# Experts 0 to 3 of a mixture of experts: one product of 448 columns where two products of 224 stood

## The chip, the cores and the metric

The kernel runs on one core of one Trainium2 chip. Its time is the device time in microseconds (us) of one execution; the figure quoted is the median of the runs, and a profiled execution of the same program gives the trace.

## What is computed

Three layers stand one behind the other: a bucketed attention, a mixture of 8 experts that gives each of 1,536 tokens to one expert, and a dense layer with an ELU. The change touches the second alone:

```python
def _moe_ref(x, w_gate, w_output_gate, w1, w2):
    logits = x @ w_gate
    e_idx = np.argmax(logits, axis=1)
    ...
    for e in range(E):
        mask = e_idx == e
        h = np.maximum(x[mask] @ w1[e], 0.0)
        ye = h @ w2[e]
        out[mask] = gate_w[mask, None] * eom[mask, e, None] * ye
    return out
```

There D = 512 and F = 1024, so w1[e] is 512 by 1024 and w2[e] is 1024 by 512. The gate factors are multiplied into the tokens before the experts.

## The kernel before

Every number that enters a matrix product is split in two, a high part rounded to the matmul's format (fp32r) and a low part that holds the rest. A product is then the sum of three: high weights by high tokens, high weights by low tokens, low weights by high tokens, all added up in one PSUM buffer.

The experts run one after the other (the loop at L1064), each on CAP = 224 columns of tokens. An expert's first layer, `moe_L1`, runs 8 times (f = 0 to 7), once for each block of 128 of its 1,024 hidden rows: 4 blocks of the inner dimension by three matmuls of 224 columns make one product of 12 matmuls. Its result lies in PSUM tile `hps` (3 buffers). ScalarE (ACT) writes its ReLU, rounded, to `hh` (L1040), and VectorE (DVE) writes the rest to `hl` (L1041). The second layer, `moe_L2`, runs 4 times (dc = 0 to 3), over 8 inner blocks each: 24 matmuls into PSUM tile `yps` (2 buffers), then ACT writes `x2h` (L1051) and DVE `x2l` (L1052). Its first product reads `hh` and `hl` of f = 7 in its last three matmuls.

The weights come in pieces of 128 by 1024 numbers, 8 to an expert. A piece is loaded into one of 6 buffers `wraw`, and `split_piece` makes its high part `wh` on ACT (L755) and its low part `wl` on DVE (L758). Program order alone sets where that stands: after every second `moe_L1` and after every `moe_L2` the piece 4 ahead is split. After dc = 1 and dc = 2 the next expert's tokens are transposed on TensorE (`xTp`, L1023) and split on ACT (L1025) and DVE (L1026). Each engine executes its own instructions in program order. From expert 4 on, DVE also has the narrowing of the last layer's weights (L693 to L697) among them; in experts 0 to 3 it does not. Expert 0's tokens are not made by `make_xT` but by `first_xT`, in two separate buffers.

Of the kernel before, what the change touches and what calls it, by code (L numbers as in the profile page):

```python
# [8 lines left out]
F32 = mybir.dt.float32  # L9
F32R = mybir.dt.float32r  # L10
BF16 = mybir.dt.bfloat16
I32 = mybir.dt.int32
AF = mybir.ActivationFunctionType
ALU = mybir.AluOpType
# [11 lines left out]
def kernel(  # L26
# [15 lines left out]
    nc = tc.nc  # L42
# [14 lines left out]
    CAP = 224  # L57
# [34 lines left out]
    FB1 = F // 128  # L92
    KD = DM // 128
# [675 lines left out]
    xT = {}  # L769
# [102 lines left out]
    for n in range(NQ + 3):  # L872
# [41 lines left out]
        if nx < NPAIR:  # L914
            if s % 3 and s < 9:
                late = prep(nx, s // 3 * 2 + s % 3 - 1)
            if s in v_at:
                i = v_at.index(s)
# [80 lines left out]
    x2h = x2_p.tile([128, KD, XW], F32R, name="x2h")  # L999
    x2l = x2_p.tile([128, KD, XW], F32R, name="x2l")  # L1000

    moe = ctx.enter_context(ExitStack())
    m1 = moe.enter_context(tc.tile_pool(name="m1", bufs=1, reuse_waits="tile"))
    ps_y = moe.enter_context(tc.tile_pool(name="ps_y", bufs=2, space=PSUM, reuse_waits="tile"))
    ps_x = moe.enter_context(tc.tile_pool(name="ps_x", bufs=2, space=PSUM, reuse_waits="tile"))
    ps_h = moe.enter_context(tc.tile_pool(name="ps_h", bufs=3, space=PSUM, reuse_waits="tile"))
# [6 lines left out]

    def make_xT(e, half):
        if half == 0:
            xT[e] = [m1.tile([128, KD, CAP], F32R, tag="xT" + x, name="xT" + x) for x in ("h", "l")]
        hi, lo = xT[e]
        t = xsl[e]
        ps = ps_x.tile([128, 2, 2, 128], F32, tag="x", name="xTp")
        for i in range(2):  # L1020
            dc = 2 * half + i
            for a in range(2):
                nc.tensor.transpose(ps[:, i, a, :], t[:, a, dc * 128:(dc + 1) * 128], ident)  # L1023
        pv = ps.rearrange("p i a q -> p i (a q)")[:, :, 0:CAP]
        nc.scalar.activation(hi[:, 2 * half:2 * half + 2], pv, AF.Copy)  # L1025
        nc.vector.tensor_tensor(lo[:, 2 * half:2 * half + 2], pv, hi[:, 2 * half:2 * half + 2], ALU.subtract)  # L1026

    hT = {}

    def moe_L1(e, f, pc):  # L1030
        if f == 0:
            hT[e] = [m1.tile([128, FB1, CAP], F32R, tag="h" + x, name="h" + x) for x in ("h", "l")]
        hi, lo = xT[e]
        wh, wl = (t.rearrange("p (c f) -> p c f", c=KD) for t in wsp[pc])
        fs = slice(f % 2 * 128, f % 2 * 128 + 128)
        ps = ps_h.tile([128, CAP], F32, tag="h", name="hps")
        for dc in range(KD):
            for i, (w, x) in enumerate(((wh, hi), (wh, lo), (wl, hi))):
                nc.tensor.matmul(ps, w[:, dc, fs], x[:, dc], start=(dc == 0 and i == 0), stop=(dc == KD - 1 and i == 2))  # L1039
        nc.scalar.activation(hT[e][0][:, f], ps, AF.Relu)  # L1040
        nc.vector.scalar_tensor_tensor(hT[e][1][:, f], ps, 0.0, hT[e][0][:, f], ALU.max, ALU.subtract)  # L1041

    def moe_L2(e, dc, pc, col):
        hi, lo = hT[e]
        wh, wl = (t.rearrange("p (c f) -> p c f", c=FB1) for t in wsp[pc])
        ps = ps_y.tile([128, CAP], F32, tag="y", name="yps")
        for f in range(FB1):
            for i, (w, x) in enumerate(((wh, hi), (wh, lo), (wl, hi))):
                nc.tensor.matmul(ps, w[:, f], x[:, f], start=(f == 0 and i == 0), stop=(f == FB1 - 1 and i == 2))  # L1049
        cols = bass.ds(col, CAP)  # L1050
        nc.scalar.activation(x2h[:, dc, cols], ps, AF.Copy)  # L1051
        nc.vector.tensor_tensor(x2l[:, dc, cols], ps, x2h[:, dc, cols], ALU.subtract)  # L1052

    more = "a count of some of the tokens"
    most = nc.values_load(
        tab[0:1, 2 * E:2 * E + 1], engines=[ENG.Pool], min_val=0, max_val=NT, skip_runtime_bounds_check_because=more
# [7 lines left out]
    for e in range(E):  # L1064
# [9 lines left out]
        for f in range(FB1):  # L1074
            pc = e * NP + f // 2
            moe_L1(e, f, pc)
            narrow_ops(1)
            if f == 1 and e + 1 < E:
                scale_xs(e + 1, (nc.gpsimd, nc.gpsimd))
            if f == 4 and e >= E - NG:  # L1080
                tids(e - E + NG)
            if f % 2:
                wsp.pop(pc)
                split_piece(pc + AHEAD)
                if e == E - 1 and f == 7:
                    split_w2(0)
                take_w2()
# [3 lines left out]
        for dc in range(KD):  # L1091
            pc = e * NP + 4 + dc
            moe_L2(e, dc, pc, off)
            narrow_ops(2)
            wsp.pop(pc)
            split_piece(pc + AHEAD)
            if e + 1 < E and dc in (1, 2):
                make_xT(e + 1, dc - 1)
            if e == E - 1 and dc == 2:
                split_w2(1)  # L1100
            take_w2()
            if dc == 2 and e + 2 < E:
                load_xs(e + 2)
# [16 lines left out]
    def ff_L1(hf, fb, j):  # L1120
        wh, wl = (t[:, 0].rearrange("p (c f) -> p c f", c=KD) for t in w2s[fb])
        c0 = hf * (NT // 2) + j * HC
        ps = ps_g.tile([128, HC], F32, tag="g", name="gps")
        for dc in range(KD):
            for i, (w, x) in enumerate(((wh, x2h), (wh, x2l), (wl, x2h))):
                nc.tensor.matmul(  # L1126
                    ps, w[:, dc], x[:, dc, c0:c0 + HC], start=(dc == 0 and i == 0), stop=(dc == KD - 1 and i == 2)
                )
        return ps
# [50 lines left out]
    for k in range(len(steps)):  # L1180
        for j in range(2):
            ps = ff_L1(*steps[k], j)
# [130 lines left out]
```

## Time and profile before

| what | value |
|---|---|
| time, median of 3 runs | 737.04 us (736.97 to 737.53) |
| the profiled execution | 736.89 us |
| its span, first to last instruction | 735.1 us |
| TensorE matmul (PE) busy | 714.1 us, 97% of the span |
| VectorE busy | 562.6 us, 77% |
| ScalarE busy | 400.3 us, 54% |
| granted TensorE clock, mean | 0.987 of full speed |

The page also cuts the span in 40 slices of 18.4 us, gives the chain of work that ended last, and lists the costliest groups of instructions. A matmul's duration of some 270 ns is the time from its start to its modelled end; matmuls overlap, so the time between two starts is what one costs. The same holds for ACT and DVE, where an instruction may start up to 0.1 us before the one ahead of it has ended.

### The profile page before, as it was taken

The numbers are of one execution on the slowest core, as the hardware profiler recorded it, in microseconds if no ns is written. First come the engines' busy times: TensorE is split into PE (matmuls) and PEld (weight loads), VectorE is DVE, ScalarE is ACT, GpSimd is POOL, SyncE is SP. The second block draws the span as 40 slices with busy tenths as digits, with TensorE's granted clock in tenths as the row PEclk, the third lists the DMA queues.
The fourth block names the chain that finished last, engine by engine and source line by source line (L and its number), as shares of the span: only waits on it lengthen the run. The fifth ranks groups of instructions, "written<-read, shape, count | busy, mean of one in ns | idle before, by whom it ended". The sixth has DMA issues, their size and how long they took to land.

```text
span 735.1 us, 13186 instructions
## 1 busy us (share of the span) xinstructions
PE 714.1 (97%) x4686; PEld 672.0 (91%) x4687; DVE 562.6 (77%) x1093; ACT 400.3 (54%) x807; POOL 206.9 (28%) x492
## 2 busy tenths in 40 slices
PE   7999999999999979999999999999999999999996
PEld 5899999999999969999999999889988999899995
DVE  5888988989889988666688987786778955964433
ACT  3887878888788855555556554333432223232221
POOL 7444444554446434202251345000000000000203
PEclk9899999999999989999999999999999999999998
DMA  8856768577682208976779997232122200000202
GB/s 189 190 112 151 186 155 207 130 171 183 159 216 90 88 0 261 290 229 181 222 236 248 219 280 201 82 104 69 58 77 68 86 1 1 1 0 1 86 1 89
DMA packets 108537, 97.76 MB, mean 133 GB/s; under 512 B 33416, under 2 KB 94472, under 8 KB 108464
## 3 DMA queue, kind: packets, MB, share of 16 engines
q1 hardware_dynamic: 106000, 90.44, 46.1%
q0 software_dynamic: 2304, 6.40, 2.3%
q8 instruction: 39, 0.64, 0.3%
q14 instruction: 34, 0.28, 0.1%
q10 hardware_dynamic: 160, 0.00, 0.0%
HBM read 64.15 MB, written 10.72 MB: 102 GB/s over the span
## 4 chain that ended last, share of the span: by engine, by line
PE 50%; issue 31%; DMA 9%; DVE 4%; ACT 3%; POOL 1%; SPq 1%; ACTq 0%; POOLq 0%; DVEq 0%
PE yps L1049 10%; PE hps L1039 10%; PE o L378 8%; PE t L362 7%; DMA out_dram<-part,tidt 6%; PE s L314 4%; PE s L315 4%; PE zps L229 2%; PE sp L454 2%; ACT p L342 1%; PE prep L203 1%; DMA tid_d<-tok,g_pi 1%; PE xTp L1023 1%; DMA qb<-qhi 1%; PE xacc L818 1%
## 5 line engine op out<-in xcount | busy, mean ns | idle before, releaser
L365 DVE TENSOR_TENSOR ptlo<-t,pthi 128x384 fp32r<-128x384 f32 x192 | 100.0, 548 | 25.9 <-ACT pthi L364 23.4
L342 ACT ACTIVATE p<-s,bi,sc 128x768 f32<-128x768 f32 x96 | 96.0, 1000 | 21.3 <-POOL bi L335 19.7
L364 ACT ACTIVATE pthi<-t 128x384 fp32r<-128x384 f32 x192 | 84.8, 497 | 25.8 <-PE t L362 24.8
L758 DVE TENSOR_TENSOR wl<-wraw,wh 128x1024 fp32r<-128x1024 f32 x63 | 77.0, 1224 | 21.2 <-ACT wh L755 16.1
L1138 ACT ACTIVATE gh<-ee 128x384 fp32r<-128x384 f32 x64 | 33.6, 525 | 108.4 <-DVE ee L1137 108.4
L333 DVE TENSOR_REDUCE nm<-s 128x1 f32<-128x768 f32 x96 | 91.0, 947 | 0.0
L1126 PE MATMUL gps<-x2h,vh 128*128 128x384 f32 x256 | 86.5, 338 | 0.0
L1126 PE MATMUL gps<-x2h,vl 128*128 128x384 f32 x256 | 86.2, 337 | 0.0
L1126 PE MATMUL gps<-x2l,vh 128*128 128x384 f32 x256 | 86.0, 336 | 0.0
L1174 POOL DMA_INDIRECT out_dram<-part,tidt x12 | 11.6, 965 | 258.6 <-DVE part L1170 256.8
L362 PE MATMUL t<-ident,p 128*128 128x128 f32 x576 | 80.9, 276 | 2.9 <-DVE ptlo L365 1.9
L314 PE MATMUL s<-ka,qa 128*128 128x384 f32 x192 | 74.5, 388 | 3.0 <-ACT p L342 2.2
L1156 PE MATMUL a<-vh,gl 128*128 128x512 f32 x192 | 75.4, 393 | 1.7 <-DVE gl L1139 1.5
L1156 PE MATMUL a<-vl,gh 128*128 128x512 f32 x192 | 75.5, 393 | 0.0
L1156 PE MATMUL a<-vh,gh 128*128 128x512 f32 x192 | 75.4, 393 | 0.0
L362 PEld LDWEIGHTS t<-ident,p 128*128 128x128 f32 x576 | 68.6, 142 | 6.8 <-DVE ptlo L365 2.3
L1049 PE MATMUL yps<-hh,wh 128*128 128x224 f32 x256 | 71.4, 279 | 0.0
L1135 ACT ACTIVATE ee<-gps 128x384 f32<-128x384 f32 x64 | 31.2, 487 | 72.6 <-PE gps L1126 72.4
L1049 PE MATMUL yps<-hl,wh 128*128 128x224 f32 x256 | 70.5, 275 | 0.0
L1049 PE MATMUL yps<-hh,wl 128*128 128x224 f32 x256 | 70.0, 273 | 0.0
L378 PE MATMUL o<-pthi,vst 128*128 128x384 f32 x192 | 68.1, 355 | 0.8 <-ACT osb L399 0.6
L315 PE MATMUL s<-kb,qb 102*128 102x384 f32 x192 | 66.0, 344 | 0.8 <-DMA qb<-qhi 0.8
(202 smaller groups left out, 1865.1 us busy)
## 6 DMA issues: line engine op xcount, KB each, us to landing
wraw<-in_moe_w_dram SPq DMA_DIRECT2D x64, 512.0 KB
w<-in_moe_w_in_dram SPq DMA_DIRECT2D x16, 512.0 KB
w<-in_moe_w_out_dram SPq DMA_DIRECT2D x16, 512.0 KB
ka<-khi SPq DMA_DIRECT2D x30, 192.0 KB
xs_d<-zt SPq DMA_DIRECT2D x8, 528.0 KB
xs<-xs_d SPq DMA_DIRECT2D x8, 528.0 KB
raw_q<-in_q_dram SPq DMA_DIRECT2D x16, 192.0 KB
raw_k<-in_k_dram SPq DMA_DIRECT2D x16, 192.0 KB
```

Source lines behind the costliest of these rows:

```text
L314: nc.tensor.matmul(ps[:, j, 0:HC], opnd[st, "qa"][:, cb], opnd[st, "ka"][:, sl], start=True, stop=False)
L315: nc.tensor.matmul(ps[:, j, 0:HC], opnd[st, "qb"][0:64 + MROWS, cb], opnd[st, "kb"][0:64 + MROWS, sl], start=False, stop=True,)
L333: nc.vector.tensor_reduce(nm, sps[n][:, :, 0:HC], AX.XY, ALU.max, negate=True)
L342: nc.scalar.activation(p.rearrange("p (a b) -> p a b", a=2), sps.pop(n)[:, :, 0:HC], AF.Exp, bias=bi, scale=sc, accum_out=sums[hd][:, c:c ...
L362: nc.tensor.transpose(ps[:, a, :], p[:, kt * 128:(kt + 1) * 128], ident)
L364: nc.scalar.activation(ho, ps, AF.Copy)
L365: nc.vector.tensor_tensor(lo[:, HALF * g:HALF * (g + 1), i * 128:(i + 1) * 128], ps, ho, ALU.subtract)
L378: nc.tensor.matmul(ops[m], vst[hd][:, kt, :], t[:, kt, :], start=(kt == 0 and x == 0), stop=(kt == NC - 1 and x == 1))
L758: fs = [lambda: eng.tensor_tensor(lo, r, hi, ALU.subtract)]
L1049: nc.tensor.matmul(ps, w[:, f], x[:, f], start=(f == 0 and i == 0), stop=(f == FB1 - 1 and i == 2))
L1126: nc.tensor.matmul(ps, w[:, dc], x[:, dc, c0:c0 + HC], start=(dc == 0 and i == 0), stop=(dc == KD - 1 and i == 2))
L1156: nc.tensor.matmul(ps, x[:, cs], w, start=(fb in first_fb and i == 0), stop=(fb in last_fb and i == 2))
```

## The change

In experts 0 to 3 the high and the low part of the tokens now lie in one tile, so that a high weight block can meet both in one matmul of 2 x 224 = 448 columns. The PSUM tile holds both halves, `ps[:, 0]` and `ps[:, 1]`; the low weight block goes into `ps[:, 0]` alone. Where three matmuls of 224 columns stood, there is one of 448 and one of 224. The two halves are then added: ACT copies `ps[:, 1]` to an SBUF tile `sum`, DVE adds `ps[:, 0]` to it, and only then follow the ReLU (or the copy) on ACT and the low part on DVE, both of them from `sum`. These last two (`rest`) are put on a list and issued at the next product, behind its copy and ahead of its add. After f = 7, and at the start of each second-layer product, the list is emptied at once.

Expert 0's first layer keeps the three matmuls, since its tokens lie in two buffers, and so do experts 4 to 7. The number of PSUM buffers is the same.

```diff
     def make_xT(e, half):
         if half == 0:
-            xT[e] = [m1.tile([128, KD, CAP], F32R, tag="xT" + x, name="xT" + x) for x in ("h", "l")]
+            t = m1.tile([128, 2, KD, CAP], F32R, tag="xT", name="xT")
+            xT[e], xB[e] = (t[:, 0], t[:, 1]), t
...
+    def settle(n):
+        while len(owed) > n:
+            owed.pop(0)()
+
+    def product(ps, w, x, n):
+        wh, wl = w
+        for k in range(n - 1):
+            nc.tensor.matmul(ps, wh(k), x[:, :, k], start=(k == 0), stop=False)
+            nc.tensor.matmul(ps[:, 0], wl(k), x[:, 0, k], start=False, stop=False)
+        nc.tensor.matmul(ps[:, 0], wl(n - 1), x[:, 0, n - 1], start=False, stop=False)
+        nc.tensor.matmul(ps, wh(n - 1), x[:, :, n - 1], start=False, stop=True)
+
+    def joined(ps):
+        t = m1.tile([128, CAP], F32, tag="sum", name="sum", bufs=4)
+        nc.scalar.activation(t, ps[:, 1], AF.Copy)
+        settle(0)
+        nc.vector.tensor_tensor(t, ps[:, 0], t, ALU.add)
+        return t
...
+        if e in JOIN and e in xB:
+            ps = ps_h.tile([128, 2, CAP], F32, tag="h", name="hps2")
+            product(ps, (lambda k: wh[:, k, fs], lambda k: wl[:, k, fs]), xB[e], KD)
+            t = joined(ps)
+
+            def rest():
+                nc.scalar.activation(h, t, AF.Relu)
+                nc.vector.scalar_tensor_tensor(l, t, 0.0, h, ALU.max, ALU.subtract)
+
+            owed.append(rest)
+            if f == FB1 - 1:
+                settle(0)
+            return
...
+        if e in JOIN:
+            ps = ps_y.tile([128, 2, CAP], F32, tag="y", name="yps2")
+            settle(0)
+            product(ps, (lambda k: wh[:, k], lambda k: wl[:, k]), hT[e], FB1)
+            t = joined(ps)
+
+            def rest():
+                nc.scalar.activation(x2h[:, dc, cols], t, AF.Copy)
+                nc.vector.tensor_tensor(x2l[:, dc, cols], t, x2h[:, dc, cols], ALU.subtract)
+
+            owed.append(rest)
+            return
...
+    JOIN = (0, 1, 2, 3)
```

On ACT, in the first layer of expert 3, four products (f = 4 to 7) and two pieces of weights stand so before the change (`x2` marks two in a row):

```order
L1040 ACTIVATE hh<-hps 128x224 x2
L755 ACTIVATE wh<-wraw 128x1024
L1040 ACTIVATE hh<-hps 128x224 x2
L755 ACTIVATE wh<-wraw 128x1024
L1051 ISA
```

and so after it (the numbers behind the names tell one product's tile from another's):

```order
L1047 ACTIVATE sum<-hps_5484 128x224
L1064 ACTIVATE h<-sum 128x224
L1047 ACTIVATE sum<-hps_5498 128x224
L1064 ACTIVATE h<-sum 128x224
L755 ACTIVATE wh<-wraw 128x1024
L1047 ACTIVATE sum<-hps_5518 128x224
L1064 ACTIVATE h<-sum 128x224
L1047 ACTIVATE sum<-hps_5532 128x224
L1064 ACTIVATE h<-sum 128x224 x2
L755 ACTIVATE wh<-wraw 128x1024
```

Two instructions stand where one stood, and the ReLU `h` behind a copy belongs to the product before; the last two ReLUs stand together. On DVE the same stretch, before:

```order
L1041 SCALAR_TENSOR_TENSOR hl<-hps,hh 128x224 x2
L758 TENSOR_TENSOR wl<-wraw,wh 128x1024
L1041 SCALAR_TENSOR_TENSOR hl<-hps,hh 128x224 x2
L758 TENSOR_TENSOR wl<-wraw,wh 128x1024
L1052 ISA
```

and its end after the change, f = 5 to 7:

```order
L1049 TENSOR_TENSOR sum<-hps_5226,sum 128x224
L758 TENSOR_TENSOR wl<-wraw,wh 128x1024
L1065 SCALAR_TENSOR_TENSOR h<-sum,h 128x224
L1049 TENSOR_TENSOR sum<-hps_5246,sum 128x224
L1065 SCALAR_TENSOR_TENSOR h<-sum,h 128x224
L1049 TENSOR_TENSOR sum<-hps_5260,sum 128x224
L1065 SCALAR_TENSOR_TENSOR h<-sum,h 128x224
L758 TENSOR_TENSOR wl<-wraw,wh 128x1024
```

Behind each `wl` the low part of the product before comes first, then the next product's add. (These are expert 2's rows; experts 1 to 3 read alike.)

## Rows read from the trace of the kernel before

**Rows 1.** Windows: length, then PE, PEld, DVE, ACT, POOL busy, clock, DMA share, GB/s

```profile
325.46:347.77 22.31, 22.31 (x203) 22.31 (x202) 15.21 (x23) 12.73 (x22) 4.57 (x2) 1.00 0.69 214
370.08:392.40 22.32, 22.32 (x202) 22.32 (x202) 19.96 (x36) 12.74 (x22) 9.65 (x8) 1.00 0.76 199
...
460.00:560.00 100.00, 98.70 (x497) 88.91 (x496) 75.98 (x147) 36.25 (x68) 0.00 (x0) 1.00 0.25 77
560.00:700.00 140.00, 139.57 (x704) 126.44 (x703) 92.82 (x178) 39.80 (x75) 6.36 (x12) 1.00 0.08 27
```

**Rows 2.** Chain of work that ended last, expert 2: start, length, what

```profile
325.46 10.72 PE hps L1039 x96
336.18 5.36 PE yps L1049 x48
341.55 0.44 PE xTp L1023 x4
341.98 2.68 PE yps L1049 x24
```

**Rows 3.** Waits from 303 to 437 us: total, times, longest

```profile
ACT x2h L1051 <- PE yps L1049: 32.8, 24, 1.4
ACT hh L1040 <- PE hps L1039: 23.6, 24, 1.0
```

**Rows 4.** Timeline of PE, experts' stage and last layer: start, length, what

```profile
325.30 0.28 PE L1039 MATMUL hps<-xTh,wh 128*128 128x224 f32 x1
...
522.15 0.33 PE L1126 MATMUL gps<-x2h,vh 128*128 128x384 f32 x1
...
524.24 0.39 PE L1156 MATMUL a<-vh,gh 128*128 128x512 f32 x1
...
526.31 0.33 PE L1126 MATMUL gps<-x2h,vh 128*128 128x384 f32 x1
```

**Rows 5.** Timeline of ACT, expert 1's end and expert 2's start

```profile
322.64 1.05 ACT L755 ACTIVATE wh<-wraw 128x1024 fp32r<-128x1024 f32 x1
323.59 0.54 ACT L1025 ACTIVATE xTh<-xTp 128x448 fp32r<-128x448 f32 x1
325.50 0.36 ACT L1051 ACTIVATE x2h<-yps 128x224 f32 x1 [1.37 <-PE yps L1049]
...
328.18 0.36 ACT L1040 ACTIVATE hh<-hps 128x224 fp32r<-128x224 f32 x1 [0.98 <-PE hps L1039]
328.43 1.05 ACT L755 ACTIVATE wh<-wraw 128x1024 fp32r<-128x1024 f32 x1
```

**Rows 6.** Timeline of DVE, first layers of experts 0 and 2

```profile
284.17 0.68 DVE L1041 SCALAR_TENSOR_TENSOR hl<-hps,hh 128x224 fp32r<-128x224 f32 x2
...
328.57 0.39 DVE L1041 SCALAR_TENSOR_TENSOR hl<-hps,hh 128x224 fp32r<-128x224 f32 x1 [0.21 <-ACT hh L1040]
329.51 1.23 DVE L758 TENSOR_TENSOR wl<-wraw,wh 128x1024 fp32r<-128x1024 f32 x1 [0.55 <-PE hps L1039]
330.66 0.38 DVE L1041 SCALAR_TENSOR_TENSOR hl<-hps,hh 128x224 fp32r<-128x224 f32 x1
```

**Rows 7.** Timeline of DVE and of ACT, last layer: ACT waits for DVE

```profile
601.67 0.56 DVE L1137 SCALAR_TENSOR_TENSOR ee<-gps,ee 128x384 f32<-128x384 f32 x1
...
602.26 0.52 ACT L1138 ACTIVATE gh<-ee 128x384 fp32r<-128x384 f32 x1 [1.02 <-DVE ee L1137]
```

**Rows 8.** Windows of 2 us ahead of the experts and in expert 0 (columns of rows 1)

```profile
270.00:272.00 2.00, 0.04 (x2) 0.00 (x0) 1.93 (x9) 0.29 (x2) 0.50 (x1) 1.00 0.00 0
272.00:274.00 2.00, 1.72 (x15) 1.72 (x15) 1.86 (x12) 1.62 (x4) 0.41 (x1) 0.65 0.00 0
274.00:276.00 2.00, 2.00 (x11) 2.00 (x11) 1.90 (x7) 1.69 (x3) 1.84 (x2) 0.50 0.03 8
...
284.00:286.00 2.00, 1.66 (x15) 1.47 (x14) 2.00 (x5) 0.62 (x2) 0.00 (x0) 1.00 0.99 305
```

More of the change, by code (lines that the diff above doesn't have):

```diff
@@ L1026, in make_xT @@
         nc.vector.tensor_tensor(lo[:, 2 * half:2 * half + 2], pv, hi[:, 2 * half:2 * half + 2], ALU.subtract)
+    xB = {}
     hT = {}
+    owed = []
+    def settle(n):
[14 more added lines that the diff above has]
+        return t
     def moe_L1(e, f, pc):
         if f == 0:
-            hT[e] = [m1.tile([128, FB1, CAP], F32R, tag="h" + x, name="h" + x) for x in ("h", "l")]
-        hi, lo = xT[e]
+            hT[e] = m1.tile([128, 2, FB1, CAP], F32R, tag="h", name="h")
         wh, wl = (t.rearrange("p (c f) -> p c f", c=KD) for t in wsp[pc])
         fs = slice(f % 2 * 128, f % 2 * 128 + 128)
+        h, l = hT[e][:, 0, f], hT[e][:, 1, f]
+        if e in JOIN and e in xB:
[9 more added lines that the diff above has]
+            return
+        hi, lo = xT[e]
         ps = ps_h.tile([128, CAP], F32, tag="h", name="hps")
@@ L1039, in moe_L1 @@
                 nc.tensor.matmul(ps, w[:, dc, fs], x[:, dc], start=(dc == 0 and i == 0), stop=(dc == KD - 1 and i == 2))
-        nc.scalar.activation(hT[e][0][:, f], ps, AF.Relu)
-        nc.vector.scalar_tensor_tensor(hT[e][1][:, f], ps, 0.0, hT[e][0][:, f], ALU.max, ALU.subtract)
+        nc.scalar.activation(h, ps, AF.Relu)
+        settle(0)
+        nc.vector.scalar_tensor_tensor(l, ps, 0.0, h, ALU.max, ALU.subtract)
     def moe_L2(e, dc, pc, col):
-        hi, lo = hT[e]
         wh, wl = (t.rearrange("p (c f) -> p c f", c=FB1) for t in wsp[pc])
+        cols = bass.ds(col, CAP)
+        if e in JOIN:
+            ps = ps_y.tile([128, 2, CAP], F32, tag="y", name="yps2")
+            settle(0)
+            product(ps, (lambda k: wh[:, k], lambda k: wl[:, k]), hT[e], FB1)
[5 more added lines that the diff above has]
+            return
         ps = ps_y.tile([128, CAP], F32, tag="y", name="yps")
         for f in range(FB1):
-            for i, (w, x) in enumerate(((wh, hi), (wh, lo), (wl, hi))):
-                nc.tensor.matmul(ps, w[:, f], x[:, f], start=(f == 0 and i == 0), stop=(f == FB1 - 1 and i == 2))
-        cols = bass.ds(col, CAP)
+            for i, (w, x) in enumerate(((wh, 0), (wh, 1), (wl, 0))):
+                nc.tensor.matmul(
+                    ps, w[:, f], hT[e][:, x, f], start=(f == 0 and i == 0), stop=(f == FB1 - 1 and i == 2)
+                )
         nc.scalar.activation(x2h[:, dc, cols], ps, AF.Copy)
+        settle(0)
         nc.vector.tensor_tensor(x2l[:, dc, cols], ps, x2h[:, dc, cols], ALU.subtract)
+    JOIN = (0, 1, 2, 3)
     more = "a count of some of the tokens"
```

## The prediction

> **What bounds the kernel now.** I read the windows first, cut at the experts' borders: what counts is whether TensorE ever stands still in the stretch that is changed. In expert 2 PE is busy for 22.31 of 22.31 us, in expert 4, which keeps its form, for 22.32 of 22.32, and in the last layer for 98.70 of 100 and 139.57 of 140 us [rows 1]. The chain of work that ended last says the same from the other side: an expert is 10.72 us of first layer, 4 x 2.68 us of second layer and 2 x 0.44 us of transposes, all of it PE, 22.31 us together [rows 2]. The waits show the others waiting for PE: of nine rows none has PE waiting, none has ACT or DVE waiting for a load, and the longest with them as waiters are ACT's for PE [rows 3]. So PE is the bound from expert 1 to the end; what the change adds to or takes from an expert reaches the end of the kernel one to one, whichever engine it comes from. ACT is busy for 12.73 us of an expert and DVE for 15.21 [rows 1].
>
> **What the product gains on PE.** A matmul of 224 columns now costs 10.72/96 = 0.1117 us [rows 2]. What 448 columns cost no row shows; it is read between two sizes that stand in the last layer: 12 of 384 columns from 522.15 to 524.24, 0.174 us each, and 9 of 512 from 524.24 to 526.31, 0.230 us each [rows 4]. The line through both gives 0.202 us at 448 and 0.104 at 224. The 224 columns cost more than the line, and transposes of 128 columns cost 0.44/4 = 0.11 us as well [rows 2], so below some 240 columns it is not the columns that set the pace but, I take it, the weight load that comes with each matmul. The change takes one load in three away. A pair then costs 0.202 + 0.112 = 0.314 us where three matmuls cost 0.335: 0.021 us less, 0.085 in a first-layer product (4 pairs, 1.255 us), 0.17 in a second-layer product (8 pairs, 2.51 us), 0.68 in a half expert. Bounds of a pair: 0.335 (nothing gained) and, with 448 columns at one a cycle of the granted 2.4 GHz (clock 1.00 in rows 1), 0.187 + 0.112 = 0.299.
>
> The Trainium skill ("TensorE: Matmul & The Clock Gate", sections "Back-to-back issue gap" and "LDWEIGHTS (loading the stationary operand)") gives N/2.4 + 2.5 ns for a matmul and 128/1.2 = 107 ns for a load, so 0.189 + 0.107 = 0.296 us for a pair, an estimate from that page. For the load the trace is close (0.11); for 384 and 512 columns, where the page has 0.163 and 0.216, the rows have 0.174 and 0.230. By the page's pair the sum below would be 1.8 us lower.
>
> **What it adds on ACT and DVE.** Each joined product gets a copy on ACT (as `x2h`, 0.36 us) and an add on DVE (as `hl`, 0.39) [rows 5, 6]. By totals that fits: 12.7 + 12 x 0.36 = 17.1 us on ACT and 15.2 + 12 x 0.39 = 19.9 on DVE, under the 20.9 us that PE would need. By order it does not. Products now go ACT, DVE, ACT, DVE instead of ACT, DVE, and the split of a weight piece stands in the same two queues. The prices: on ACT the next instruction starts 0.25 us after a small one (328.18 to 328.43) and a split `wh` takes 1.05 [rows 5]; on DVE the next starts 1.15 after a `wl` (329.51 to 330.66) and 0.68 - 0.39 = 0.29 after a small one [rows 6]; ACT to DVE takes 0.03 (328.54 to 328.57) [rows 5, 6] and DVE to ACT 0.03 (602.23 to 602.26) [rows 7].
>
> In the first layer, from one even ReLU to the next but one (f = 0, 2, 4, 6): ReLU of f, 0.25; `wh` behind it on ACT, 1.05; hand over, 0.03; `wl`, 1.15; low part of f+1, 0.29; add of f+2, 0.39; hand over, 0.03; then ReLU of f+2. That is 3.19 us for two products. PE would need 2.51, and needs 2.68 today. So the first layers of experts 1 to 3 are no longer bound by PE but by this ring; today it does not exist, since `hh` waits only for PE.
>
> **The sum for experts 1 to 3.** Time 0 is the first matmul of the first layer. ACT sees the end of the product before at 0.20 (325.30 to 325.50 [rows 4, 5]): copy at 0.20, `wh` 0.45 to 1.50, `wl` at 1.53, the low part owed at 2.68, add of f = 0 at 2.97 to 3.36, its ReLU at 3.39. Three rounds of 3.19 bring the ReLU of f = 6 to 12.96. Its low part follows at 13.35, the add of f = 7 at 13.64, its ReLU at 14.06, its low part at 14.45, done at 14.84. The last matmul of the first second-layer product needs it: 0.03 to hand over, 0.11 to load, 0.20 to stream, so the second product starts at 15.18. Today it is 10.72 + 2.68 = 13.40: **1.78 us later**. PE stands in the meantime, first for an `hps` buffer (three, freed by the adds: f = 5 and f = 7 wait, 0.3 and 0.7 us), then for `h` of f = 6 and 7 (0.8 us each). The other three second-layer products have time: 2.51 us on PE against 1.15 + 2 x 0.29 + 0.53 (`xTl`) on DVE. They gain 3 x 0.17 = 0.51. Net +1.27 us for each of three experts, **+3.81**.
>
> **Expert 0** joins only its second layer, whose hidden rows come from the old form; it gains 4 x 0.17 = **-0.68**. Later experts run as before: the last product's owed copy and subtraction fall into gaps that ACT and DVE have. Loads see an expert that is longer, not shorter, so nothing there comes late. The swapped order of a product's last two matmuls costs nothing. Sum: +3.13 us on the profiled 736.89, 740.0; the median lies 0.15 above that run, so **740.2**.
>
> The open prices: 104 pairs run free of the ring (3 x 24 and 32), so a pair's bounds move the sum by -1.6 and +2.2 us. Some 12 handovers lie on an expert's path; at 0 or 0.06 us instead of 0.03 they move it by 0.36 each way, 1.1 for three. Both together reach from 737.5 to 743.5.
>
> **The rivals.** (1) *PE keeps the bound.* If ACT and DVE let ring and splits overlap better than their rows show, seven half experts gain 0.68 each: 4.8 us, 732.2. For it speak the totals, 17.1 and 19.9 under 20.9 us; against it, that every step of the ring is a wait for data or a place in a queue. It decides once the ring takes less than 2.51 us, a fifth less than the rows add up to. 8%. (2) *448 columns run at the bare column rate*, a pair at 0.299: -1.6 on the forecast, 738.6, with cheaper handovers down to 737.5. Rows at 384 and 512 columns speak against it. 15%. The page's two rules above are this case, at 738.3. (3) *The change does not do what it says:* the second load was never the limit, or two token blocks in one matmul cost extra, and a pair stays at 0.335. Then +2.2, 742.4. 8%. (4) *The clock falls* where PE now waits. After 270 to 272 us, with 0.04 us of work, the clock was 0.65 and 0.50 in the next two windows, 1.2 GHz for some 3.4 us; in 284 to 286, with 1.66 us of work, it stayed at 2.4 GHz [rows 8]. The new gaps are below 1 us each, nearer to the second row. If it fell once in each of experts 1 to 3, half the speed for 3.4 us would cost 1.7 us each: 745.3. 7%.
>
> **How the numbers follow.** The forecast has 62%. The range, 737.3 to 743.6, takes in rivals 2 and 3 and leaves out 1 and 4, 15%. A measurement of this kernel can tell 0.2%, 1.5 us, from no change. Faster: rival 1 and a little of the low ends, 0.09. Same, up to 738.5: half of rival 2 and the forecast's low edge, 0.14. Slower: 0.77.
>
> **What would show it.** In experts 1 to 3 of the changed kernel: 23.6 us from one first layer to the next; ReLUs of even f 3.2 us apart; PE waiting for DVE, 2 to 3 us an expert, most of it in the first second-layer product; 448-column matmuls whose pair takes 0.314 us where nothing waits; expert 0's second layer 0.7 us shorter; experts 4 to 7 at 22.3; clock 1.00 throughout. An expert of 20.9 us with no PE wait would make it wrong.

## The result and the profile after

The changed kernel takes **741.66 us** (median; 740.71 to 742.4) beside 737.0 for the kernel before on the same chip (736.36 to 737.53): a ratio of **1.0063**, 95% interval 1.005 to 1.0076. That is 4.66 us slower. The forecast was 740.2 with a range of 737.3 to 743.6, so sign and range hold, and the size is short by a third.

Windows of the changed kernel, cut at the first matmul of each expert's first layer, experts 0 to 4 (columns as in [rows 1]):

```profile
280.76:303.28 22.52, 22.18 (x171) 21.37 (x170) 17.82 (x27) 14.89 (x26) 5.26 (x6) 1.00 0.98 288
303.28:327.18 23.90, 22.51 (x138) 20.05 (x137) 18.82 (x35) 16.21 (x34) 4.13 (x2) 1.00 0.71 215
327.18:351.30 24.12, 22.38 (x137) 20.04 (x136) 18.81 (x35) 16.15 (x34) 3.47 (x2) 1.00 0.64 196
351.30:375.43 24.13, 22.39 (x138) 20.06 (x136) 18.81 (x35) 16.15 (x34) 3.63 (x2) 1.00 0.65 197
375.43:397.73 22.30, 22.30 (x202) 22.30 (x200) 20.66 (x38) 12.99 (x23) 8.42 (x8) 1.00 0.79 203
```

Experts 1 to 3 take 23.90, 24.12 and 24.13 us, 72.15 together, where the kernel before takes 22.31 for each, 66.93 (expert 2 in [rows 2]; experts 1 and 3 read alike): **+5.2**. Expert 0 takes 22.52 where it took 23.1 (279.89 to 302.99 in PE's timeline of before): **-0.6**. All of that lies in its second layer, 11.01 us instead of 11.58; its first layer takes 11.5 in both traces, though up to 12.55 in the traces of kernels below that leave it as it is. Expert 4 keeps its three matmuls, and its time too, although in the changed kernel its tokens and hidden rows also lie in joined tiles, as those of experts 5 to 7 do; so the tiles by themselves cost nothing there. The two differences make +4.6, nearly the whole change of the median. (The profiled execution took 742.4, and its experts start 0.87 us later than in the trace of before, ahead of anything that was changed.) No engine is full in experts 1 to 3: PE is busy for 22.4 of 24.1 us, DVE for 18.8, ACT for 16.2. What bounds such a stretch is an order of waits, and the chain shows it.

Chain of work that ended last in the changed kernel, expert 2, one round of the first layer and the tail behind it (start, length, what; "issue" is time in which the engine waited for nothing that the profile shows):

```profile
337.27 0.03 ACT h L1064
337.30 0.27 issue
337.57 1.05 ACT wh L755
338.62 0.02 issue
338.64 1.23 DVE wl L758
339.87 0.30 DVE h L1065
340.17 0.31 DVE sum L1049
340.49 0.02 issue
340.51 0.40 ACT h L1064
...
341.66 0.40 ACT h L1064
342.06 0.02 issue
342.08 0.40 DVE h L1065
...
342.53 0.47 PE yps L1043
```

Where [rows 2] have nothing but PE, PE comes in here only at 342.53. The ring of the prediction stands there link by link: ReLU, `wh`, `wl`, low part, add, and the next even ReLU 3.24 us later. The even ReLUs of the whole first layer (ACT's timeline, same expert):

```profile
330.64 0.39 ACT L1064 ACTIVATE h<-sum 128x224 fp32r<-128x224 f32 x1 [0.31 <-DVE sum L1049]
...
333.87 0.39 ACT L1064 ACTIVATE h<-sum 128x224 fp32r<-128x224 f32 x1 [1.03 <-DVE sum L1049]
...
337.27 0.39 ACT L1064 ACTIVATE h<-sum 128x224 fp32r<-128x224 f32 x1 [1.29 <-DVE sum L1049]
...
340.51 0.39 ACT L1064 ACTIVATE h<-sum 128x224 fp32r<-128x224 f32 x1 [1.12 <-DVE sum L1049]
```

Rounds of 3.23, 3.40 and 3.24 us, each ended by a wait for DVE's add. In [rows 3] ACT waits for PE alone. The round of 3.40 has one longer split in it (DVE's timeline):

```profile
332.01 1.23 DVE L758 TENSOR_TENSOR wl<-wraw,wh 128x1024 fp32r<-128x1024 f32 x1 [0.26 <-ACT wh L755]
...
335.25 1.38 DVE L758 TENSOR_TENSOR wl<-wraw,wh 128x1024 fp32r<-128x1024 f32 x1 [0.27 <-ACT wh L755]
```

PE's timeline of the changed kernel shows what a pair costs and where PE stands (same expert):

```profile
330.97 0.36 PE L1040 MATMUL hps<-xT,wh 128*128 128x448 f32 x1
331.17 0.26 PE L1041 MATMUL hps<-xT,wl 128*128 128x224 f32 x1
331.27 0.38 PE L1040 MATMUL hps<-xT,wh 128*128 128x448 f32 x1
...
332.23 0.37 PE L1040 MATMUL hps<-xT,wh 128*128 128x448 f32 x1
...
333.99 0.45 PE L1040 MATMUL hps<-xT,wh 128*128 128x448 f32 x1 [0.33 <-DVE sum L1049]
...
337.39 0.45 PE L1040 MATMUL hps<-xT,wh 128*128 128x448 f32 x1 [0.64 <-DVE sum L1049]
...
341.38 0.47 PE L1040 MATMUL yps<-h,wh 128*128 128x448 f32 x1 [0.57 <-DVE h L1065]
```

From 330.97 to 332.23 four pairs run without a wait, 0.315 us each. Then PE waits for an `hps` buffer and at last for `h`.

### The profile page after: what moved, and what is told of

It is laid out like the page before. It is cut to its first block, busy times and chain, and to the rows that moved or that the text cites. A ratio compares the mean times of both kernels' runs of the same rounds, so it can differ in the third digit from the quotient of the medians.

```text
span 740.7 us, 12841 instructions
## 1 busy us (share of the span) xinstructions
PE 712.9 (96%) x4462; PEld 663.2 (90%) x4463; DVE 573.8 (77%) x1133; ACT 411.9 (56%) x847; POOL 207.1 (28%) x492
## 4 chain that ended last, share of the span: by engine, by line
PE 41%; issue 31%; DMA 10%; DVE 8%; ACT 6%; POOL 2%; SPq 2%; ACTq 0%; POOLq 0%; DVEq 0%
PE o L378 7%; DMA out_dram<-part,tidt 6%; PE t L362 6%; PE hps L1075 5%; PE yps L1098 4%; PE s L314 4%; PE s L315 3%; PE yps L1040 2%; DVE wl L758 2%; ACT wh L755 2%; PE zps L229 2%; ACT p L342 2%; PE sp L454 2%; PE yps L1041 1%; SPq L132 1%
## 5 line engine op out<-in xcount | busy, mean ns | idle before, releaser
L755 ACT ACTIVATE wh<-wraw 128x1024 fp32r<-128x1024 f32 x63 | 66.0, 1051 | 0.7 <-DMA wraw<-in_moe_w_dram 0.5
L378 PE MATMUL o<-ptlo,vst 128*128 128x384 f32 x192 | 64.9, 338 | 0.0
L778 POOL TENSOR_SCALAR xs<-xs 128x512 f32<-128x512 f32 x14 | 29.3, 2103 | 115.0 <-DMA xs<-xs_d 115.0
```

The source lines that it names most:

```text
L378: nc.tensor.matmul(ops[m], vst[hd][:, kt, :], t[:, kt, :], start=(kt == 0 and x == 0), stop=(kt == NC - 1 and x == 1))
L755: eng_hi.activation(hi, r, AF.Copy)
```

## The experiments

The theory is the ring: a joined product goes to ACT, DVE, ACT and DVE, and with the split of a weight piece in the same two queues it comes round too late for PE. The rivals: the joined matmuls themselves cost more (load, columns, PSUM); GpSimd or the total load of VectorE does it. The kernels were run in three groups, each beside runs of the kernel before, whose medians were 737.38, 737.75 and 736.95; each ratio is to those of its own group.

### Each half alone

The second layer alone:

```
-        if e in JOIN and e in xB:
+        if False:
```

> Only the second layers of experts 0 to 3 are joined; the first layers keep three matmuls of 224 columns and two evacuation steps. Ring theory (the loss sits in the first layers, where copy, ReLU and weight split on ScalarE and low part, add and weight split on VectorE wait for each other in turn): no ring, PE without a wait, four half experts gain 4 x 0.17 us each, 16 x 0.17 = 2.7 us less than before: 734.3 us. Load theory (VectorE and ScalarE simply have too much to do): 4 x 0.39 us more on VectorE, 16.8 us of some 21.6, also no loss. Rival that joining itself costs (the matmul over two token blocks, the adds): 737 or above.

Measured: 734.58 (734.42 to 734.62), ratio 0.9961, 0.9947 to 0.9974. The window of expert 1 (2 and 3 read alike):

```profile
302.46:324.18 21.72, 21.72 (x170) 21.13 (x169) 16.24 (x27) 13.86 (x26) 4.85 (x2) 1.00 0.82 247
```

As expected of it (734.3). PE has no idle time again, and an expert takes 0.59 us less than before: 32 pairs, 0.0185 us each. So the joined product does save time on PE, and the loss must come from the first layer. The first layer alone:

```
-        if e in JOIN:
+        if False:
```

> Only the first layers of experts 1 to 3 are joined; all second layers keep their three matmuls. Ring theory: the first layer and the first second-layer product take 15.4 to 15.7 us as in the changed kernel, where 13.4 stood before, and nothing is gained in the other second-layer products: 2.0 to 2.3 us more for each of three experts, 743.1 to 743.8 us, slower than the full change. Load theory: 8 x 0.39 us more on VectorE, 18.3 of 22.3 us, fits: about 735.

Measured: 742.59 (742.5 to 743.38), ratio 1.0074, 1.006 to 1.0088; experts 1 and 2 take 24.04 and 24.22 us (expert 3 24.20). The ring had put it at 743.1 or above, the load at 735: the ring theory holds, half a microsecond milder. The two halves do not add up. Joining the second layer saves 0.59 us an expert by itself, but behind a joined first layer only 0.14 and 0.10 us (23.90 and 24.12 against 24.04 and 24.22). ACT's timeline of this kernel shows the first ReLU of expert 2:

```profile
330.12 0.39 ACT L1064 ACTIVATE h<-sum 128x224 fp32r<-128x224 f32 x1
```

That is 3.10 us behind the first matmul (327.02); in the changed kernel it is 3.46 (327.18 to 330.64). There the last second-layer product owes DVE a low part, and `x2l` stands ahead of the add:

```profile
329.92 0.38 DVE L1091 TENSOR_TENSOR x2l<-sum,x2h 128x224 f32 x1
330.22 0.39 DVE L1049 TENSOR_TENSOR sum<-hps,sum 128x224 f32<-128x224 f32 x1
```

That puts 0.30 us ahead of the ring, and 0.06 more come from ACT's first copy, which starts 0.26 us after the first matmul (327.18 to 327.44) instead of 0.20 (327.02 to 327.22), behind a last matmul of 448 columns instead of 224. So 0.36 us of what PE gains in three second-layer products goes into the start of the next ring.

### Two products owed instead of one

If the ring binds, letting the ReLU and the low part of a product come one product later takes the add out of their line, with the same instructions:

```
-    def joined(ps):
+    def joined(ps, n=0):
...
-        settle(0)
+        settle(n)
...
-            t = joined(ps)
+            t = joined(ps, 1)
```

(The last line is the first layer's call.)

> The full change, with one number altered: in the first layer the ReLU and the low part of a product are issued two products later instead of one (until f = 7, where all are issued). The same instructions on every engine, in another order. Ring theory: the ReLU of f waits for an add that was done a whole product earlier, so the ring spans three products instead of two and its 3.2 us fit in 3 x 1.25; PE is the bound again but for the end at f = 7, an expert takes 21.3 to 21.4 us: 3.5 us less than before, 733.5 us. Load theory: the load is the same, so the time stays at 741.7.

Measured: 734.98 (733.76 to 736.12), ratio 0.997, 0.996 to 0.9981. Experts 1 to 3 take 21.76, 21.66 and 21.66 us; the waits of PE from 300 to 368 us are down to these (PEld is its weight load):

```profile
PEld yps L1040 <- DVE h L1065: 0.9, 3, 0.3
PEld hps L1040 <- issue: 0.5, 3, 0.2
```

This is the clearest of the runs. Matmuls, copies and adds are all there; only the order in two queues differs, and 2.1 to 2.5 us per expert go. It is 1.5 us short of the 733.5 expected of it: PE still waits for low parts of the last products. That these stand behind a `wl`, and that two low parts are stretched (below), are likely reasons.

### One split moved

In experts 1 to 3 the piece that is split behind f = 5 is split behind f = 7 instead:

```
-                split_piece(pc + AHEAD)
+                if e in (1, 2, 3) and f == 7:
+                    split_piece(pc - 1 + AHEAD)
+                if e not in (1, 2, 3) or f != 5:
+                    split_piece(pc + AHEAD)
```

> The full change; in experts 1 to 3 the weight piece that is split after f = 5 is split after f = 7 instead, ahead of the piece that stands there. The same instructions on the same engines, none on GpSimd more. Ring theory with the split as its longest part: the round from the ReLU of f = 4 to that of f = 6 loses 1.05 us on ScalarE and 1.15 us on VectorE and falls from 3.23 us to what PE needs or a little above, 2.5 to 2.6; two splits in a row behind f = 7 stand behind the last low part and delay nobody before the second layer's second product. About 0.6 to 0.7 us less for each of three experts than the full change, 1.8 to 2.1 in all: 739.7 us. Theory of the chain without the split (ReLU, low part, add and three handovers alone bind): the round stays at 3.2 and the time at 741.7.

Measured: 739.86 (739.0 to 740.36), ratio 1.0032, 1.002 to 1.0044, as the ring had it (739.7); experts of 23.25, 23.30 and 23.31 us. The round without a split (DVE's timeline, expert 2):

```profile
335.78 0.39 DVE L1065 SCALAR_TENSOR_TENSOR h<-sum,h 128x224 fp32r<-128x224 f32 x1 [0.46 <-ACT h L1064]
336.09 0.38 DVE L1049 TENSOR_TENSOR sum<-hps,sum 128x224 f32<-128x224 f32 x1
336.93 0.39 DVE L1065 SCALAR_TENSOR_TENSOR h<-sum,h 128x224 fp32r<-128x224 f32 x1 [0.46 <-ACT h L1064]
```

A product goes round in 1.15 us, two in 2.30, where PE needs 2.52. Without a split the ring is shorter than PE's work; with one it is 0.7 us longer. Both edits together:

> The full change with both alterations: in the first layer the ReLU and the low part of a product come two products later, and in experts 1 to 3 the piece split after f = 5 is split after f = 7. With the deferral alone PE still waits some 0.4 us in the first second-layer product and 0.15 before it, for the low parts of f = 6 and 7, which stand behind a 1.15 us split on VectorE. Ring theory: without that split ahead of them they are early enough, PE stands nowhere in experts 1 to 3, an expert takes 8 x 1.26 + 4 x 2.53 + 0.88 = 21.1 us instead of 21.7: 1.7 us less than with the deferral alone, about 733.2 us, the fastest of all. If the end of the first layer is bound by the handovers alone, the same as the deferral alone, 735.0.

Measured: 734.62 (733.88 to 736.24), ratio 0.9965, 0.9952 to 0.9978; experts of 21.54, 21.56 and 21.61 us. They would be 21.1 with no wait at all (22.31 less twice 0.59), so 0.4 to 0.5 us stays in each. The expectation, 733.2, was missed: the median can't be told from that with two products owed alone; in the experts it is 0.37 us for the three (64.71 against 65.08), where 1.7 had been expected. So the split was not what held up most of the rest. The other expectation, that the handovers at the end of the first layer bind, is the nearer one: in expert 2, PE goes on at 336.11 and 336.66 us, 0.06 behind the ends of the low parts of f = 6 and 7 (336.05 and 336.60 in DVE's timeline).

### The split on GpSimd

```
-                split_piece(pc + AHEAD)
+                split_piece(pc + AHEAD, nc.gpsimd if e in (1, 2, 3) and f > 4 else nc.vector)
```

> The full change, with the low parts of two of the four weight pieces that are split in the first layers of experts 1 to 3 (after f = 5 and f = 7) made by GpSimd instead of VectorE. Ring theory: one round of three loses its 1.15 us split on VectorE and falls to what PE needs, 2.5 instead of 3.2 us; the split after f = 7 lies behind the last low part and gives nothing: about 0.6 us less for each of three experts, 739.9 us. Load theory: VectorE has 2.5 us less in each expert, so up to 2.5 us an expert come back, 734 or less. Rival that GpSimd slows VectorE where both write at once: 741 or above.

Measured: 749.4 (746.58 to 750.6), ratio 1.017, 1.0156 to 1.0183: a miss by 9.5 us against the ring's 739.9, and of the three expectations the last, that GpSimd slows VectorE, comes nearest. POOL's and DVE's timelines in expert 2 (of the fastest execution):

```profile
338.78 2.39 POOL L758 TENSOR_TENSOR wl<-wraw,wh 128x1024 fp32r<-128x1024 f32 x1 [2.26 <-ACT wh L755]
```

```profile
339.25 2.17 DVE L1065 SCALAR_TENSOR_TENSOR h<-sum,h 128x224 fp32r<-128x224 f32 x1 [0.78 <-ACT h L1064]
341.34 0.38 DVE L1049 TENSOR_TENSOR sum<-hps,sum 128x224 f32<-128x224 f32 x1
```

The low part that began while GpSimd split took 2.17 us instead of 0.39 and ended 0.25 us after GpSimd. The split had left VectorE's queue, but it held VectorE up all the same. In expert 3, PE's granted clock fell as well (0.64 in 368 to 370 us, 0.50 in 370 to 372), and the second layer took 15.07 us instead of the 13.72 of expert 2. The run says nothing against the ring; as a remedy it costs more than it gives.

### A link of the ring doubled

The low part of a joined first-layer product is issued twice, which adds a small DVE instruction at one known place:

```
+                nc.vector.scalar_tensor_tensor(l, t, 0.0, h, ALU.max, ALU.subtract)
```

> The full change, with the low part of each joined first-layer product written twice by VectorE (the second time the same numbers). Ring theory: each round has one low part in it, so a round grows by the 0.30 us after which VectorE takes the next small instruction, 3.23 to 3.53; three rounds give 0.9, and two low parts at the end of the first layer 0.3 to 0.6 more: 1.2 to 1.5 us for each of three experts, 745.3 to 746.2 us. Theory that PE is the bound outside the first second-layer product: 0.3 to 0.6 an expert, 743.

Measured: 753.17 (750.19 to 756.3), ratio 1.0215, 1.0191 to 1.024: slower as the ring says, but 7 us above what was expected of it, so it does not confirm the size. DVE's timeline in expert 2:

```profile
341.51 0.39 DVE L1065 SCALAR_TENSOR_TENSOR h<-sum,h 128x224 fp32r<-128x224 f32 x1 [0.46 <-ACT h L1064]
341.94 0.39 DVE L1066 SCALAR_TENSOR_TENSOR h<-sum,h 128x224 fp32r<-128x224 f32 x1
342.25 0.38 DVE L1049 TENSOR_TENSOR sum<-hps,sum 128x224 f32<-128x224 f32 x1
342.55 1.21 DVE L758 TENSOR_TENSOR wl<-wraw,wh 128x1024 fp32r<-128x1024 f32 x1
```

The second low part writes what the first one writes and starts only 0.43 us after it, 0.04 behind its end, where an independent one starts after 0.30. DVE's queue now sets the round, with one ReLU on ACT in it: ReLU 0.42, low parts 0.43 and 0.31, add 0.30, split 1.13, low parts 0.42 and 0.31, add 0.41, together 3.73, as from 341.09 to 344.82 in ACT's timeline. The expectation had taken 0.30 for the new instruction once and missed this path. The round ahead of it took 4.13 us (336.96 to 341.09), with a low part of 0.78. Windows of experts 2 and 3, and inside expert 3:

```profile
329.48:356.47 26.99, 22.97 (x137) 20.06 (x136) 22.27 (x43) 16.25 (x34) 4.25 (x2) 1.00 0.57 178
356.47:386.06 29.59, 25.87 (x138) 22.60 (x136) 22.06 (x43) 16.24 (x34) 4.19 (x2) 0.88 0.53 164
372.00:374.00 2.00, 0.95 (x3) 0.48 (x3) 1.48 (x5) 0.88 (x2) 0.00 (x0) 0.94 0.75 234
374.00:376.00 2.00, 1.58 (x5) 1.45 (x6) 1.87 (x3) 1.21 (x3) 0.00 (x0) 0.50 0.00 0
```

Expert 2 takes 2.9 us more than in the changed kernel, expert 1 as much (26.79). In expert 3 another 2.9 come from the clock: after PE has waited for the ring (busy for 0.95 of the 2 us from 372 on) the clock is down to 0.50 of full speed, 1.2 GHz, from about 374 to 380 us. A second-layer product takes 4.69 us there (374.96 to 379.65) where 2.5 is usual, and the whole second layer 16.79 us instead of the 13.92 of expert 2, where the clock stayed at 1.00. The fastest execution, 750.19, has a mean clock of 0.988, the slowest, 756.3, one of 0.980.

### Without the scaling on GpSimd

```
-            if f == 1 and e + 1 < E:
+            if f == 1 and e + 1 < E and e + 1 not in (2, 3, 4):
```

> The full change without the GpSimd multiplications of the tokens of experts 2, 3 and 4 by their gate factors, which are left out (those experts' outputs lack the factor). In experts 2 and 3 of the full change one weight split on VectorE takes 1.38 us instead of 1.23 while GpSimd multiplies. If GpSimd's work stretches it, all splits now take 1.23, all rounds 3.23, and the way from first layer to first layer falls from 24.12 to 23.9 us in experts 2 and 3. If not, one split of 1.38 stays.

One run, 741.56. DVE's timeline of expert 2, the split of the same piece that took 1.38:

```profile
334.66 1.23 DVE L758 TENSOR_TENSOR wl<-wraw,wh 128x1024 fp32r<-128x1024 f32 x1 [0.26 <-ACT wh L755]
```

All splits of experts 1 and 2 are back at 1.23, and they take 23.91 and 23.97 us instead of 23.90 and 24.12. So the stretched split is GpSimd's doing, and it is worth 0.15 us where it falls into the ring, not more; the rest of the loss stays without GpSimd. (One run doesn't place the whole time against 741.66.)

### The second layer of more experts

The second layer alone, taken on to experts 0 to 6, as the version to beat:

```
-    JOIN = (0, 1, 2, 3)
+    JOIN = tuple(range(E - 1))
```

> The first layers are in the old form in all experts; the joined second layer is taken to experts 0 to 6. Theory (a joined second-layer product has time on ACT and DVE, so its 8 pairs give what they give on TensorE): experts 4, 5 and 6 come down from 22.3 to 21.7 us each, as experts 1 to 3 do where the second layer alone is joined, so 1.8 us below that kernel's 734.6: 732.8. Rival (VectorE becomes the bound there): in experts 4 and 5 of the kernel before it is busy for 20.0 to 20.2 of 22.3 us with the last layer's weights; four adds of 0.39 us more make 21.6 to 21.7 of the 21.7 us that TensorE needs, so any idle time on VectorE becomes a wait of TensorE, and these experts stay at 22.3 us or above: 734.6 or more.

> The first layers are in the old form, the second layers of experts 0 to 3 joined; run again for the comparison with the same form in experts 0 to 6. Both theories: 734.6, as before.

Measured: 734.45 (733.33 to 736.83), ratio 0.9967, 0.9958 to 0.9976, and for experts 0 to 3 again 734.41 (733.73 to 735.14), ratio 0.9965, 0.9952 to 0.9977. There is no difference. Windows of experts 4 to 6:

```profile
366.70:388.42 21.72, 21.72 (x171) 21.14 (x170) 20.66 (x39) 13.85 (x26) 9.62 (x8) 1.00 0.74 207
388.42:410.43 22.01, 21.98 (x171) 21.22 (x170) 20.91 (x40) 13.96 (x26) 8.35 (x8) 1.00 0.99 281
410.43:432.73 22.30, 21.97 (x170) 21.22 (x170) 21.16 (x40) 14.04 (x26) 7.89 (x8) 1.00 1.00 260
```

Expert 4 gains the 0.59 us, the next ones less and nothing, as DVE fills up to 21.2 of 22.3 us. Expert 7, whose form is the same in both kernels, takes 22.01 us (432.57 to 454.58) instead of 21.44 in the run beside it, which gives most of that back. PE waits at the start of the next first layer:

```profile
411.53 0.37 PE L1075 MATMUL hps<-xT,wh 128*128 128x224 f32 x1 [0.33 <-DVE xT L1027]
```

The same wait stands at 433.83. It is for the low part of the next expert's tokens, which stands in DVE's full queue. Here the rival of that run was right: VectorE becomes the bound.

## Why the prediction was right, and where it was short

**PE was the bound, and what an expert gains or loses reaches the end one to one.** Right: +5.2 and -0.6 in the experts, +4.66 in the median.

**The pair at 0.314.** Right: 0.315 in the rows above. The second layer alone shows the gain without the ring, in both its runs: 0.59 us for 32 pairs, where 0.68 were booked. The estimate of 0.296 from the Trainium skill ("TensorE: Matmul & The Clock Gate", "Back-to-back issue gap" and "LDWEIGHTS (loading the stationary operand)") does not agree with the trace; the line through the rows at 384 and 512 columns does. So rival 2 falls, and rival 3 with it: a pair at 0.335 would have shown no gain in the second layer.

**The ring.** Right as a mechanism: the chain shows its links in the order given, PE's waits fall where they were put (0.33 and 0.64 for an `hps` buffer against 0.3 and 0.7; the `h` of f = 6 and 7 after that), and most of it goes when a product is owed longer. It was mis-sized, by 0.32, 0.54 and 0.55 us in the three experts, 1.41 together, nearly the whole miss (expert 0 adds 0.1). For expert 2: the rounds took 9.87 instead of 9.57, the start to the first ReLU 3.46 instead of 3.39 (the copy starts at 0.26, not at the 0.20 that was read behind a matmul of 224 columns), from the last even ReLU to the second product of the second layer 2.33 (340.51 to 342.84) instead of 2.22, the rest 8.46 instead of 8.41. Two terms make up the rounds. The ReLU was priced by one that reads PSUM ([rows 5]: 0.36, the next after 0.25); it now reads `sum` in SBUF, takes 0.39 and lets the next start after 0.30 (333.87 to 334.17 in ACT's timeline): 0.05 a round. And GpSimd's scaling stretches one split by 0.15. The rows that were read did not show this: the split of [rows 6] started at 329.51, 0.69 us ahead of such a multiplication (330.20 in POOL's timeline of before), and took 1.23. In the same trace a split that started inside one (309.89; GpSimd from 309.42) took 1.30.

**Expert 0 at -0.68.** Right in kind, measured -0.6. It is the same term as the second layer alone.

**Rival 1**, PE keeping the bound, was turned down because each link is a wait for data or a place in a queue. That held for this order. The experiments show that the order decides, not the totals: with the same work and two products owed, PE stands still for about half a microsecond an expert. **Rival 4**, the clock, did not come up in the changed kernel: 1.00 in every window of its experts. But it was no empty rival. With longer waits of PE, with the low part written twice and with the split on GpSimd, the clock did fall in expert 3; there it cost 2.9 and 1.35 us, where 1.7 had been put on one fall.

One thing the sum held without pointing it out: its 3.39 us to the first ReLU have the owed low part of the last second-layer product in them. Without a joined second layer they are 3.10. So of the 0.51 us booked for the second layer more than half goes back into the next ring, and the effects of the two halves do not add up.

Two forms are faster than both kernels by a little over 0.3%: the second layer alone (734.6 and 734.4 in experts 0 to 3, 734.45 in 0 to 6), and the full change with two products owed (735.0, and 734.6 with a split moved as well). The second form joins three more half experts and gets no more out of them.

## What to carry over

When an evacuation becomes a chain across two engines, write out one round of both queues with everything else that stands in them, and compare that round with PE's time for the same products; totals of 16 and 19 us under 21 said nothing. If the round is longer, owe its later links for one product more before taking work out. Price each new link by a row with the same operands in the same memories, and look at what runs on GpSimd beside it. Where PE is made to wait longer, look at the granted clock too: in two of these kernels its fall came on top of the waits.

## What was not expected of the hardware

GpSimd holds VectorE up. With GpSimd splitting a piece, a VectorE low part of 0.39 us took 2.17; with GpSimd scaling tokens (3.5 to 5.3 us), splits took 1.38 instead of 1.23 and low parts 0.49 and 0.58. DVE's timeline in the kernel with two products owed, while GpSimd scaled (329.32 to 333.37):

```profile
329.40 0.38 DVE L1049 TENSOR_TENSOR sum<-hps,sum 128x224 f32<-128x224 f32 x1
329.70 0.58 DVE L1065 SCALAR_TENSOR_TENSOR h<-sum,h 128x224 fp32r<-128x224 f32 x1
330.20 0.38 DVE L1049 TENSOR_TENSOR sum<-hps,sum 128x224 f32<-128x224 f32 x1
```

The low part reads two operands in SBUF and is stretched; the add reads one in PSUM and keeps its 0.38. In the kernel before, the low part read PSUM too ([rows 6], `hl<-hps,hh`), and none of the 27 from 300 to 376 us took more than 0.393, so the change has also opened its low parts to this. The Trainium skill ("SBUF — State Buffer", "Who interferes with whom") says that a VectorE instruction with two SBUF inputs contends with a GpSimd instruction that reads SBUF, while one with at most one SBUF input, outside the two-port modes, does not. The rows above agree. Not every such instruction is stretched: in the kernel before, a split that started at 332.19, beside a multiplication from 332.15 on, kept 1.22.
